# Heads laid out as 64 partitions of seven rows, with all attention products in quarters of the array

## The chip, the cores and the metric

The kernel runs on one core of one Trainium2 chip. TensorE multiplies matrices on a 128 x 128 array, VectorE (DVE), ScalarE (ACT) and GpSimd (POOL) work on vectors, and SyncE (SP) issues transfers, which sixteen DMA engines carry out. Each engine works through its instructions in order. The metric is device time in microseconds (us), from the start of an execution to its end. Lower is better.

## The reference

Attention for 8 batches of 12 heads with a sigmoid in place of a softmax, and then a gated feed-forward block over all 3584 tokens:

```python
# q, k, v: (8, 12, 448, 64)
scores = q @ k^T / sqrt(64) - log(448)
attn = 1 / (1 + exp(-scores))
x = (attn @ v), heads put side by side    # (3584, 768)
g = x @ w_gate                            # (768, 1536)
h = g * sigmoid(g) * (x @ w_val)
out = h @ w_out                           # (3584, 768)
```

A head has 448 rows, which is three and a half times 128, or seven times 64. Keys can be taken in any order, as long as k and v have the same one, and so can queries, as long as the rows of the output are put back where they belong.

## The kernel before, in words

Work is cut into 24 items of four heads: item i holds group i mod 3 of batch i div 3. For an item, q, k and v are loaded as float32 by SP, cast to 16 bits (by DVE for items 0 to 2, by POOL later), and q and k are transposed, for items 0 to 5 on TensorE (L371, copied out of PSUM by DVE at L377) and from item 6 on by a DMA transpose that SP issues (L387).

The first 384 rows of a head lie as 128 partitions of three rows (`load_main`, L261). The last 64 rows, the tails, are loaded apart (`tails`, L221 and L242): five DMAs for every item of batches 0 and 1, and nine in one block for a whole later batch. Their casts go to places in the tile `src16` that was set to zero at the start (L183), so that two heads' tails share one tile with zeros in the unused quarters.

Scores are computed with the keys on the partitions. One tile holds the scores of 128 keys of two heads against all 448 queries: two matmuls in the two row halves of the array (L411, `burst`), each with 64 rows of contraction, 128 columns of weights and 448 columns that stream. Six such tiles, and one tile for the tails of four heads from two full-array matmuls (L426, `burst_tail`), make an item. ScalarE applies the sigmoid to each tile (L434), seven per item. Values (`pv`) take 12 matmuls in the two column halves of the array (L447) and four in its quarters for the tails (L455). The result is copied from PSUM as `xT`, already transposed for what follows.

The feed-forward part runs per batch over twelve column blocks f (`f1`, L493, six matmuls each for the gate and the value), then per pair of batches over 14 units (`f2`, L551, twelve matmuls of 384 columns each). Weights are loaded by SP in four chunks w0 to w3 of six DMAs (L331), and w_out as twelve DMAs (wo, L354), and cast by POOL.

The order of the work is written by a planner inside the program (`list_schedule`). Operations are listed item by item, in four slots sl 0 to 3 per item, each with an engine, a planned duration and what it depends on. The planner walks through time, lets each engine take the first ready operation of a window (40 operations on PE, 8 on POOL, 1 on SP), and the instructions are then written out in that order. On the chip, an engine doesn't leave its order: an instruction that isn't ready holds all behind it. A planned DMA takes `n / 16 * max(0.042, 0.0105 + size / 27200)` us for n pieces of size bytes, one after the other, and lands 2.2 us later. SP's order of loads at the start is ORDER, q1 q2 w0 q3 w1 q4 w2 q5 w3 q6, where q1 stands for q, k and v of item 1. Later, item i's slot 1 brings the transpose of item i + 2, the loads of item i + 3, and for i from 4 to 7 three loads of wo. From item 3 on an item brings feed-forward products: three each for items 3 to 6, later up to two per slot.

Buffers are rings with a number of places: ten float32 loads (`st`), two of `src`, three of the transposed `qkT`, ten of sigmoid results (`pt`), and in PSUM two score tiles (A), two banks for transposes and values (TO), two for feed-forward products (G).

Of the kernel before, what the change touches and what calls it, by code (L numbers as in the profile page):

```python
# [25 lines left out]
class Op:  # L26


    def __init__(self, eng, dur, fn, deps=(), mode=("F", "F"), take=(), give=(), desc=(0, 0)):
        self.eng, self.dur, self.fn, self.mode = eng, dur, fn, mode  # L30
        self.deps = [d for d in deps if d is not None]
        self.take = [Slot(t) for t in take]
        self.give = list(give)
        self.rank = self.t0 = self.t1 = None
        n, size = desc
        self.hold = n == 2048
        self.dma = 2.2 if n == 2048 else n / 16 * max(0.042, 0.0105 + size / 27200)
# [97 lines left out]
def kernel(  # L135
# [17 lines left out]
    SM = 384  # L153
    ST = S - SM
    NS = SM // 128
# [14 lines left out]
    slots = {"A": 2, "TO": 2, "G": 2, "st": 10, "sq": 2, "sk": 2, "sv": 2, "src": 2,  # L170
# [6 lines left out]
    src16 = [one.tile([128, 2, 8, 128], BF16, tag=f"src{i}", name=f"src{i}") for i in range(NSRC)]  # L177
    NVB = 3
    vt16 = [one.tile([128, 2, D], FP16, tag=f"vt{i}", name=f"vt{i}") for i in range(NVB)]
    nc.gpsimd.memset(sb_t, sbias)  # L180
    make_identity(nc, idn)
    for t in src16:
        nc.vector.memset(t, 0.0)  # L183
# [27 lines left out]
    def tails(b, rs, eng="SP"):  # L211

        h0, h1 = 4 * rs[0], 4 * rs[-1] + 4
        first = rs[0] == 0
        nh = h1 - h0

        def qpart():
            if first:
                T["sq", b] = stg.tile([128, H, D], FP32, tag="sq", bufs=2, name=f"sq{b}")
            r = slice(0, 64) if b % 2 == 0 else slice(64, 128)  # L220
            (nc.scalar if eng == "ACT" else nc.sync).dma_start(  # L221
                out=T["sq", b][r, h0:h1], in_=q[b][h0:h1, SM:S, :].rearrange("h p d -> p h d"))
        a = op(eng, 0.6, qpart, take=["sq"] if first else [], desc=(64 * nh, D * 4))
        if first:
            R["sq", b, "slot"] = a.take
        for r in rs:
            R["sq", b * QB + r] = [a]

        def part(nm, src, hp, e, eng):
            n = len(rs)  # L230

            def fn():
                if hp == 0 and e in (None, 0) and first:
                    T[nm, b] = stg.tile([128, QB, 2, D], FP32, tag=nm, bufs=2, name=f"{nm}{b}")
                o = T[nm, b][64 * hp:64 * hp + 64, rs[0]:rs[-1] + 1]
                hs = slice(0, 4, 3) if hp == 0 else slice(1, 3)
                i_ = src[b][h0:h1, SM:S, :].rearrange("(r f) p d -> p r f d", f=4)[:, :, hs, :]
                if n == 1:
                    o, i_ = o[:, 0], i_[:, 0]
                else:  # L240
                    o, i_ = o[:, :, e], i_[:, :, e]
                (nc.scalar if eng == "ACT" else nc.sync).dma_start(out=o, in_=i_)  # L242
            return op(eng, 0.6, fn, take=[nm] if hp == 0 and e in (None, 0) and first else [],
                      desc=(64 * n * (2 if e is None else 1), D * 4))
        for nm, src in (("sk", k), ("sv", v)):
            g = eng if nm == "sk" else "SP"
            a = [part(nm, src, hp, e, g) for hp in range(2) for e in ((None,) if len(rs) == 1 else (0, 1))]
            if first:
                R[nm, b, "slot"] = a[0].take
            for r in rs:  # L250
                R[nm, b * QB + r] = a

    def load_main(i, nm, src, part=None):
        b, r = divmod(i, QB)

        def fn():
            if part in (None, 0):
                T["st_" + nm, i] = stg.tile([128, 4, NS, D], FP32, tag="st", bufs=10,
                                            name=f"st_{nm}{i}")
            h0, h1 = (0, 4) if part is None else (2 * part, 2 * part + 2)  # L260
            nc.sync.dma_start(  # L261
                out=T["st_" + nm, i][:, h0:h1],
                in_=src[b][4 * r + h0:4 * r + h1, 0:SM, :].rearrange("h (p s) d -> p h (s d)", s=NS))
        n = 4 if part is None else 2
        R["st_" + nm, i, part] = op("SP", 0.5, fn, take=["st"] if part in (None, 0) else [],
                                    desc=(128 * n, NS * D * 4))

    def groups(b, nm):

        if nm == "k":  # L270
            return 0, 3
        return (4, 7) if b % 2 == 0 else (5, 4)

    def cast_qk(i, nm, pp, eng):
        g = groups(i // QB, nm)[0]

        def fn():
            o = src16[i % NSRC][:, pp, g:g + NS, :].rearrange("p s (h d) -> p s h d", h=2)
            cp(eng, o, T["st_" + nm, i][:, 2 * pp:2 * pp + 2].rearrange("p h s d -> p s h d"))
        ld = R.get(("st_" + nm, i, None)) or R["st_" + nm, i, pp]  # L280
        ld0 = R.get(("st_" + nm, i, None)) or R["st_" + nm, i, 0]
        R["c" + nm, i, pp] = op(eng, 0.55 if eng == "DVE" else 0.48, fn, deps=[ld], take=["src"] if nm == "q" and pp == 0 else [],
                                give=ld0.take if pp else [])

    def cast_v(i, eng, part=None):
        def fn():
            if part in (None, 0):
                T["v16", i] = sb.tile([128, 4, NS, D], FP16, tag="v16", bufs=slots["v16"],
                                      name=f"v16_{i}")
            h0, h1 = (0, 4) if part is None else (2 * part, 2 * part + 2)  # L290
            cp(eng, T["v16", i][:, h0:h1], T["st_v", i][:, h0:h1])
        last = part in (None, 1)
        R["v16", i, part] = op(
            eng, 0.83 if part is None else 0.43, fn, deps=[R["st_v", i, part]],
            take=["v16"] if part in (None, 0) else [],
            give=(R.get(("st_v", i, None)) or R["st_v", i, 0]).take if last else [])

    def cast_tails(i, eng="POOL"):
        b, r = divmod(i, QB)
        gq, gk = groups(b, "q")[1], groups(b, "k")[1]  # L300

        def fq():
            ps = slice(0, 64) if b % 2 == 0 else slice(64, 128)
            cp(eng, src16[i % NSRC][ps, :, gq, :],
               T["sq", b][ps, 4 * r:4 * r + 4, :].rearrange("p (a h) d -> p a (h d)", a=2))

        def fk():
            for rh in range(2):
                ps = slice(64 * rh, 64 * rh + 64)
                for pp in range(2):  # L310
                    hp = rh ^ pp
                    cp(eng, src16[i % NSRC][ps, pp, gk, 64 * hp:64 * hp + 64],
                       T["sk", b][ps, r, pp, :])
        free = r == QB - 1
        R["tails", i] = [
            op(eng, 0.36, fq, deps=R["sq", i] + [R["cq", i, 0]], give=R["sq", b, "slot"] if free else []),
            op(eng, 0.8, fk, deps=R["sk", i] + [R["cq", i, 0]], give=R["sk", b, "slot"] if free else [])]

    def cast_vtail(i):
        b, r = divmod(i, QB)  # L320

        def fvt():
            nc.gpsimd.tensor_copy(out=vt16[i % NVB], in_=T["sv", b][:, r])
        R["vbd", i] = op("POOL", 0.3, fvt,
                         deps=R["sv", i] + ([R["pv", i - NVB]] if i >= NVB else []),
                         give=R["sv", b, "slot"] if r == QB - 1 else [])

    def load_w(w, dst, c, j2, nm):
        def fl():
            T[nm, c, j2] = stg.tile([128, 2, CW], FP32, tag="st", bufs=10, name=f"st_{nm}{c}_{j2}")  # L330
            nc.sync.dma_start(  # L331
                out=T[nm, c, j2],
                in_=w[j2 * 256:(j2 + 1) * 256, c * CW:(c + 1) * CW].rearrange(
                    "(j p) f -> p j f", p=128))
# [16 lines left out]
    def load_wo(f):  # L351
        def fl():
            T["wo", f] = stg.tile([128, DM], FP32, tag="st", bufs=10, name=f"st_wo{f}")
# [9 lines left out]
    def qkT_tile(i):  # L363
        T["qkT", i] = sb.tile([128, 2, 8 * 128], BF16, tag="qkT", bufs=slots["qkT"], name=f"qkT_{i}")

    def tr_pe(i, pp):

        def fpe():
            ps = T["tr", i, pp] = psum.tile([128, 8 * 128], BF16, tag="TO", bufs=2, name="ps_tr")
            for g in range(8):  # L370
                nc.tensor.transpose(out=ps[:, g * 128:(g + 1) * 128],  # L371
                                    in_=src16[i % NSRC][:, pp, g, :], identity=idn)

        def fm():
            if pp == 0:
                qkT_tile(i)
# [378 lines left out]
```

## Time and profile before

| what | value |
|---|---|
| median of three runs | 454.06 us (452.81 to 454.94) |
| the profiled execution's own time | 452.38 us |
| its span in the profile | 450.6 us |
| TensorE clock granted | 1.0 |
| PE busy | 431.1 us, 96% of the span |
| ACT / DVE / POOL busy | 224.6 / 173.6 / 134.4 us |
| DMA packets | 106656, of which 59520 under 512 B |
| read from HBM, written | 47.19 MB, 11.01 MB |

The profile describes one execution. A group of instructions has its busy time, the mean duration of one, and the idle time of its engine just ahead of it with what ended that. Matmuls overlap in the array, so the duration of one (about 350 ns for 448 columns) is longer than the step from one start to the next; the steps are what count. The chain of waits is followed back from the last instruction, each time to whatever released the one before. "Landing" is the time from the issue of a transfer to its arrival.

### The profile page before, as it was taken

Reading aid. Unit: us, or ns where it says so; the run is one execution under the profiler, and the core shown is the slowest. Engines: PE = TensorE matmul, PEld = TensorE weight load, DVE = VectorE, ACT = ScalarE, POOL = GpSimd, SP = SyncE. Lnnn points to the kernel's source line nnn. Section 1 sums busy time; section 2 is a strip of 40 time slices with the busy share of each in tenths; the row PEclk is TensorE's granted clock in tenths of the full one; section 3 lists DMA queues with packets and bytes.
Section 4 is the critical chain, followed back from the end, with each engine's and each line's share of the span. In section 5 each row is a group of like instructions: output and inputs, shape, how many; then the busy total and the mean of one; then the engine's idle time right before and its main releaser. Section 6 shows DMA issues by size and latency. Waiting matters only on the chain.

```text
span 450.6 us, 6887 instructions
## 1 busy us (share of the span) xinstructions
PE 431.1 (96%) x2640; PEld 209.7 (47%) x2640; DVE 173.6 (39%) x289; ACT 224.6 (50%) x304; POOL 134.4 (30%) x313
## 2 busy tenths in 40 slices
PE   3789999999899999999999999999999999999996
PEld 1334444444354444544445444444455445554563
DVE  4525554444334334334343333433433333334210
ACT  3787753677645465454663455554743643112111
POOL 3468563554742431344033303413100000000000
PEclk9999999999999999999999999999999999999999
DMA  6999896999977678765584627616300001010032
GB/s 158 322 339 277 250 276 169 289 250 240 280 177 215 153 188 133 185 167 166 103 178 146 153 72 203 185 29 162 81 36 1 36 35 36 35 71 0 36 105 105
DMA packets 106656, 68.08 MB, mean 151 GB/s; under 512 B 59520, under 2 KB 102784, under 8 KB 106624
## 3 DMA queue, kind: packets, MB, share of 16 engines
q1 hardware_dynamic: 104576, 60.44, 50.6%
q0 software_dynamic: 1488, 7.08, 4.8%
q8 instruction: 20, 0.33, 0.3%
q10 hardware_dynamic: 560, 0.13, 0.1%
q14 instruction: 12, 0.10, 0.1%
HBM read 47.19 MB, written 11.01 MB: 129 GB/s over the span
## 4 chain that ended last, share of the span: by engine, by line
PE 72%; DMA 17%; SPq 4%; POOL 2%; issue 1%; DVE 1%; ACT 1%; POOLq 0%
PE ps_o L551 19%; PE ps_g L493 18%; PE ps_v L493 18%; DMA st_wv<-in_moe_w_val_dram 6%; PE ps_ol L551 5%; PE ps_sc L411 5%; PE ps_pv L447 4%; DMA st_q<-in_q_dram 3%; DMA st_wo<-in_moe_w_out_dram 3%; DMA sv<-in_v_dram 2%; SPq L242 2%; POOL src L205 1%; DMA st_wg<-in_moe_w_gate_dram 1%; PE ps_sct L426 1%; SPq L261 1%
## 5 line engine op out<-in xcount | busy, mean ns | idle before, releaser
L434 ACT ACTIVATE pt<-ps_sc,sbiast 128x896 f16<-128x896 f32 x144 | 136.9, 1006 | 18.6 <-PE ps_sc L411 18.5
L493 PE MATMUL ps_g<-xT,wg 128*128 128x448 f16 x576 | 124.9, 353 | 1.7 <-DVE t L503 1.5
L493 PE MATMUL ps_v<-xT,wv 128*128 128x448 f16 x576 | 125.6, 353 | 0.5 <-POOL wv L337 0.5
L499 ACT ACTIVATE s<-ps_g 128x448 f16<-128x448 f32 x96 | 52.3, 545 | 128.9 <-PE ps_g L493 125.6
L503 DVE TENSOR_TENSOR t<-ps_g,s 128x448 f16<-128x448 f32 x96 | 59.9, 624 | 140.5 <-ACT s L499 140.3
L551 PE MATMUL ps_o<-wo,hT 128*128 128x384 f16 x528 | 92.3, 326 | 0.0
L551 PEld LDWEIGHTS <-hT 128*128 128x128 f16 x672 | 65.7, 98 | 45.9 <-issue 0.4
L493 PEld LDWEIGHTS <-wg 128*128 128x128 f16 x576 | 55.3, 98 | 56.3 <-issue 8.0
L493 PEld LDWEIGHTS <-wv 128*128 128x128 f16 x576 | 51.5, 98 | 60.8 <-issue 18.8
L509 DVE SCALAR_TENSOR_TENSOR hT<-ps_v,t 128x448 f16<-128x448 f32 x96 | 60.0, 625 | 51.1 <-PE ps_v L493 49.0
L411 PE MATMUL ps_sc<-qkT 64*128 64x448 bf16 x288 | 42.5, 364 | 5.5 <-ACT pt L434 2.9
L205 POOL CAST src<-st_q 128x384 bf16<-128x384 f32 x42 | 20.5, 510 | 90.0 <-DMA st_q<-in_q_dram 83.3
L447 PE MATMUL ps_pv<-pt,v 128*64 128x448 f16 x288 | 33.4, 362 | 0.6 <-ACT pt L434 0.6
L562 ACT ACTIVATE osb<-ps_o 128x384 f32<-128x384 f32 x22 | 10.8, 491 | 43.0 <-PE ps_o L551 43.0
L203 DVE CAST xT<-ps_pv 128x448 f16<-128x448 f32 x40 | 23.6, 620 | 20.0 <-PE ps_pv L455 20.0
L205 POOL CAST v<-st_v 128x768 f16<-128x768 f32 (+1 forms) x25 | 20.0, 801 | 25.6 <-issue 15.0
L434 ACT ACTIVATE pt<-ps_sct,sbiast 128x896 f16<-128x896 f32 x24 | 24.1, 1004 | 6.3 <-PE ps_sct L426 6.3
L564 DVE TENSOR_SCALAR osb<-ps_o 128x384 f32<-128x384 f32 x22 | 12.3, 557 | 36.6 <-PE ps_o L551 36.6
L576 POOL DMA_DIRECT2D out_dram<-osb x15 | 8.3, 555 | 57.6 <-DVE osb L564 38.4
L411 PEld LDWEIGHTS <-qkT 64*128 64x128 bf16 x288 | 9.1, 94 | 34.1 <-issue 30.2
L551 PE MATMUL ps_ol<-wo,hT 128*128 128x384 f16 x144 | 24.7, 326 | 0.0
L447 PEld LDWEIGHTS <-v 128*64 128x64 f16 x288 | 14.3, 110 | 17.3 <-issue 10.1
(34 smaller groups left out, 163.2 us busy)
## 6 DMA issues: line engine op xcount, KB each, us to landing
st_q<-in_q_dram SPq DMA_DIRECT2D x23, 384.0 KB, 4.0
st_k<-in_k_dram SPq DMA_DIRECT2D x23, 384.0 KB, 4.5
st_v<-in_v_dram SPq DMA_DIRECT2D x23, 384.0 KB, 5.2
out_dram<-osb POOLq DMA_DIRECT2D x15, 384.0 KB, 2.9
st_wg<-in_moe_w_gate_dram SPq DMA_DIRECT2D x12, 384.0 KB, 6.5
st_wv<-in_moe_w_val_dram SPq DMA_DIRECT2D x12, 384.0 KB, 8.3
st_wo<-in_moe_w_out_dram SPq DMA_DIRECT2D x12, 384.0 KB, 6.6
out_dram<-osb SPq DMA_DIRECT2D x8, 384.0 KB, 2.3
```

The source lines that it names most:

```text
L203: nc.vector.tensor_copy(out=o, in_=i)
L205: nc.gpsimd.tensor_copy(out=o, in_=i)
L411: nc.tensor.matmul(out=sc[:, hp, 0:S], lhsT=kT[r, s * 128:(s + 1) * 128], rhs=qT[r, :], start=True, stop=True)
L434: nc.scalar.activation(out=pt, in_=T[("sc",) + key][:, :, 0:S], func=SIGM, bias=sb_t, scale=qkscale)
L447: nc.tensor.matmul(out=ps[64 * hp:64 * hp + 64, :], lhsT=T["v16", i][:, 2 * pp + hp, s, :], rhs=T["pt", i, pp, s][:, hp, :], start=(s == 0 ...
L493: nc.tensor.matmul(out=T[nm, b, f], lhsT=w[c][:, j, ff * 128:(ff + 1) * 128], rhs=T["xT", b, j], start=(j == 0), stop=(j == KC - 1))
L499: nc.scalar.activation(out=t, in_=T["g", b, f], func=SIGM)
L503: nc.vector.tensor_tensor(out=t, in0=T["g", b, f], in1=T["s16", b, f], op=MULT)
L509: nc.vector.scalar_tensor_tensor(out=T["hT", m, f][:, o * S:(o + 1) * S], in0=T["v", b, f], scalar=HSC, in1=T["t1", b, f], op0=MULT, op1=MULT)
L551: nc.tensor.matmul(out=o, lhsT=T["hT", m, f][:, t * 128:(t + 1) * 128], rhs=wo16[f][:, cs], start=(f == 0), stop=(f == NF - 1))
L562: nc.scalar.activation(out=T["osb", m, t][:, c], in_=o, func=COPY, scale=HREC)
L564: nc.vector.tensor_scalar_mul(T["osb", m, t][:, c], o, HREC)
```

## The change

A head's 448 rows now lie as 64 partitions of seven rows: row 7p + s of the head is at partition p, slot s. Two heads lie on partitions 0 to 63 and two on 64 to 127. There are no tails, no zeroed places, and no separate tile for them.

- Loads: q, k and v of an item take two DMAs each, one for each half of the partitions, with pieces of 1792 bytes.
- Casts: one per tensor and item instead of two, plus those of the tails; for item 0 they are split by slots between DVE and ACT.
- Transposes: seven 128 x 128 blocks for q and seven for k, each on its own, instead of eight for each pair of heads; the DMA transpose has 1792 pieces instead of 2048.
- Scores: a tile holds one slot s of the keys of all four heads. Four matmuls in the array's four quarters fill it. There are seven tiles per item, all of one kind, and from item 3 on they are issued in pairs; as seven is odd, two items share seven pairs, one of which takes the last tile of one item and the first of the next.
- Values: four matmuls in the quarters for each of seven slots.
- Output: a tile of 128 tokens is stored by two DMAs of 64 partitions.

```diff
-        self.hold = n == 2048
-        self.dma = 2.2 if n == 2048 else n / 16 * max(0.042, 0.0105 + size / 27200)
+        self.hold = n == 1792
+        self.dma = 2.0 if n == 1792 else n / 16 * max(0.042, 0.0105 + size / 27200)
...
-    slots = {"A": 2, "TO": 2, "G": 2, "st": 10, "sq": 2, "sk": 2, "sv": 2, "src": 2,
+    slots = {"A": 2, "TO": 2, "G": 2, "st": 11, "src": 2,
              "v16": 3, "qkT": 3, "pt": 10, "xT": 14, "osb": 2}
...
-    for t in src16:
-        nc.vector.memset(t, 0.0)
...
+    def load(i, nm, src):
+
+        b, r = divmod(i, QB)
+
+        def part(g):
             def fn():
...
+                if g == 0:
+                    T["st_" + nm, i] = stg.tile([128, 2, NS, D], FP32, tag="st", bufs=slots["st"],
+                                                name=f"st_{nm}{i}")
+                h = 4 * r + 2 * g
+                nc.sync.dma_start(
+                    out=T["st_" + nm, i][64 * g:64 * g + 64],
+                    in_=src[b][h:h + 2].rearrange("a (p s) d -> p a s d", s=NS))
+            return op("SP", 0.5, fn, take=["st"] if g == 0 else [], desc=(128, NS * D * 4))
+        R["st_" + nm, i] = [part(0), part(1)]
...
+    def burst(ds):
+
 
         def fpe():
-            for pp, s in ds:
+            for i, s in ds:
                 sc = psum.tile([128, 2, 512], FP32, tag="A", bufs=2, name="ps_sc")
...
+                qT, kT = T["qkT", i][:, 0], T["qkT", i][:, 1]
+                for g in range(2):
+                    for a in range(2):
+                        r = slice(64 * a, 64 * a + 64)
+                        nc.tensor.matmul(
+                            out=sc[64 * g:64 * g + 64, a, 0:S].rearrange("k (s p) -> k s p", s=NS),
+                            lhsT=kT[r, s, 64 * g:64 * g + 64], rhs=qT[r, :, 64 * g:64 * g + 64],
+                            start=True, stop=True)
...
-    def burst_tail(i):
...
+                for s in range(s0, s1):
+                    for g in range(2):
+                        for a in range(2):
+                            nc.tensor.matmul(
+                                out=T["pv", i, g][64 * a:64 * a + 64, :],
+                                lhsT=T["v16", i][64 * g:64 * g + 64, a, s, :],
+                                rhs=T["pt", i, s][64 * g:64 * g + 64, a, :],
+                                start=(s == 0), stop=(s == NS - 1))
...
+                for n in range(2):
+                    bb, s = divmod(2 * t + n, NS)
+                    rows = slice((2 * m + bb) * S, (2 * m + bb + 1) * S)
+                    dma.dma_start(out=out[rows, c].rearrange("(p s) d -> s p d", s=NS)[s],
+                                  in_=T["osb", m, t][64 * n:64 * n + 64, c])
...
+    loads(0)
+    op("ACT", 1.5, lambda: nc.scalar.activation(out=warm, in_=sb_t, func=SIGM))
+    cast_qk(0, "q", None, [("DVE", 0, 4), ("ACT", 4, NS)])
+    tr_pe(0, 0)
+    cast_qk(0, "k", None, [("DVE", 0, 4), ("ACT", 4, NS)])
+    tr_pe(0, 1)
+    cast_v(0, "POOL")
...
+    def bursts(i, sl):
+
+        if i >= NQ:
+            return []
+        if i < QB:
+            return [[(i, s)] for s in range(2 * sl, min(2 * sl + 2, NS))]
+        if (i - QB) % 2 == 0 and i + 1 < NQ:
+            return [[(i, 2 * sl), (i, 2 * sl + 1)]] if sl < 3 else [[(i, 6), (i + 1, 0)]]
+        if (i - QB) % 2 == 0:
+            return [[(i, s) for s in range(2 * sl, min(2 * sl + 2, NS))]]
+        return [[(i, 2 * sl + 1), (i, 2 * sl + 2)]] if sl < 3 else []
```

## The prediction

> **What bounds the kernel now.** I read the chain of waits first, to see what kind of work ends last, then a table of stretches, then the order of matmuls on TensorE.
>
> ```profile
> PE 72%; DMA 17%; SPq 4%; POOL 2%; issue 1%; DVE 1%; ACT 1%; POOLq 0%
> ```
>
> ```profile
> 33.00:87.00 54.00, 52.33 (x340) 24.70 (x341) 27.10 (x45) 32.20 (x44) 34.34 (x68) 1.00 0.89 254
> 87.00:115.00 28.00, 26.45 (x170) 11.24 (x167) 12.77 (x21) 20.54 (x26) 14.27 (x30) 1.00 0.92 240
> 115.00:375.00 260.00, 259.69 (x1576) 125.37 (x1577) 96.88 (x160) 137.18 (x186) 69.86 (x175) 1.00 0.52 132
> ```
>
> In the stretches (length, busy PE, PEld, DVE, ACT, POOL, clock, DMA share, GB/s) TensorE is full from 115 us on, with DMA at half. Before 115 us DMA is at 0.9: there TensorE is full only because products of the feed-forward part stand in the gaps that late attention leaves. DMA and TensorE bound that stretch together. At 113 us the products run out, and the chain in order of time shows TensorE held by a transpose that stood behind loads in SP's queue:
>
> ```profile
> 104.47 5.57 DMA st_wo<-in_moe_w_out_dram
> 110.04 5.08 DMA qkT<-src
> 115.11 0.05 issue
> 115.16 0.38 PE ps_sc L411 x2
> ```
>
> Inside the full stretch, TensorE in order of time:
>
> ```profile
> 154.50 0.54 PE L426 MATMUL ps_sct<-qkT 128*128 128x448 bf16 x2
> 154.88 1.30 PE L493 MATMUL ps_v<-xT,wv 128*128 128x448 f16 x6
> 156.02 1.30 PE L493 MATMUL ps_g<-xT,wg 128*128 128x448 f16 x6
> 157.25 0.55 PE L411 MATMUL ps_sc<-qkT 64*128 64x448 bf16 x4
> 157.73 1.31 PE L493 MATMUL ps_v<-xT,wv 128*128 128x448 f16 x6
> ```
>
> A full-array matmul of 448 columns takes a step of 0.189 us (0.38 for the two tail products). Four half-array score matmuls take 157.73 - 157.25 = 0.48 for two steps: two halves run at once. The product before should have ended at 156.02 + 6 x 0.189 = 157.15, so the change of array shape costs 0.10 going in and 0.10 coming out, plus 0.01 at each first step: 0.21 per burst.
>
> **What the Trainium skill says.** TensorEngine Tiling (Array Packing), Key Properties: changing the tiling mode drains the array. The trace agrees, at about 0.095 us a change. TensorE: Matmul & The Clock Gate, Part 3, says that weights load under running matmuls only where the row group differs; the trace differs: the full-height column halves of L447 load under running matmuls and hold steps of 0.189 to 0.190. SBUF — State Buffer, Door 1 (the port swizzle): partitions 0 to 63 reach 8 of 16 DMA ports, so 64 partitions move 196 GB/s against 328 for 128 at 1 MiB, and two transfers to the two halves together are only 6% faster. The trace has this only for stores:
>
> ```profile
> out_dram<-osb POOLq DMA_DIRECT2D x15, 384.0 KB, 2.9
> out_dram<-osb POOLq DMA_DIRECT2D x6, 192.0 KB, 3.7
> ```
>
> ```profile
> 440.40:441.40 1.00, 1.00 (x8) 0.59 (x6) 0.00 (x0) 0.49 (x1) 0.00 (x0) 1.00 0.94 372
> 436.90:438.40 1.50, 1.50 (x11) 0.92 (x10) 0.00 (x0) 0.49 (x1) 0.00 (x0) 1.00 0.97 246
> ```
>
> Half the bytes take longer to land when they leave 64 partitions, and SP's stores move 372 GB/s from 128 partitions but 246 where the tile goes out in two halves (packets of 3072 B take a median 214 ns there, 124 in the other).
>
> **The change, part by part.**
>
> Scores. Before, one item has six half-array steps and two tail steps; after, seven quarter-array steps: 0.189 us less. Only L455 runs in quarters before:
>
> ```profile
> L447 PE MATMUL ps_pv<-pt,v 128*64 128x448 f16 x288 | 33.4, 362 | 0.6 <-ACT pt L434 0.6
> L455 PE MATMUL ps_pv<-pt,vt 64*64 64x448 f16 x96 | 9.2, 373 | 0.0
> ```
>
> Its four matmuls start within 10 ns; from their start to the next full product is 0.316 us = 0.189 + 0.095 drain + 0.03. So I take 0.189 per step and 0.23 per burst. A run of several quarter steps is not shown; below zero is excluded, since every step still streams 448 columns; above, 0.024 per step (the delay of the first column-split step, 0.213 against 0.189) would cost 336 x 0.024 = 8 us, and weights that cannot load ahead (about 0.10) 34 us. I take 0, as L447 loads ahead.
>
> Bursts. Three per item before plus a tail burst without a change of shape; after 3.5. Shape changes for scores: 3.5 x 0.23 - 3 x 0.21 = +0.17. Values: seven steps both times, but three shape changes become two: a lone block costs 0.353 above its steps before and 0.23 after, -0.12. Where scores and values stand side by side (ten blocks before) they now share the shape, about -0.1 more. Sum per item -0.189 + 0.17 - 0.12 - 0.05 = about -0.2 us. For the 15 items whose scores start after 115 us: -3.0 us.
>
> Loads. One item's q, k and v are 1.376 MB. Before: 1536 packets of 768 B at a median 36 ns and 768 of 256 B at 18 (the trace's packet records), over 16 engines: 3.5 + 0.9 = 4.4 us, 4.7 with their spread. After: 768 packets of 1792 B, all to 64 partitions. From above, the full rate seen for weight loads, 375 GB/s, gives 3.7 us; from below, 218 GB/s (eight ports, the page's asymptote) gives 6.3. I take 231 GB/s, the stores' 393 KB in 1.7 us: 5.96 us. SP issues six DMAs per item; before, three, plus five for each item of the first two batches or nine once per later batch: about 6 per item as well, but the block of nine (97.4 to 102.7 us, DMA share about 0.4) is gone. The DMA transpose shrinks from 2048 to 1792 packets, some 0.3 us.
>
> Start. With first packets at 1.7 us, item 0's k lands near 6.4 instead of 4.7; cast, seven transposes and copy bring the first sigmoid to about 9.5 instead of 7.65. But then no second half is waited for, and 21 sigmoids at 0.96 to 1.0 end near 31, before 31.9: about -0.7, used up by the next item.
>
> Loads against the written order. The planner prices such a load at 8 x 0.0764 = 0.611 us, 3.67 an item, and fixes TensorE's order by it; I take 2.3 us more. Landing times, adding 5.96 per item and 6.3 per weight chunk (six of 1.05) in ORDER from 1.7: k4 42.2, k5 54.4, the last weights 62.7, k6 66.6. With 0.7 landing and 0.94 cast, the transposes of item 4 can end on TensorE at about 44, where the planner's sum has the cast near 34.5, a few us after item 3 starts. TensorE stands in order behind them: products, scores and the values of the item before, which also wait through the new burst that pairs an item's last tile with the next item's first. From item 6 on: its casts end at 68.3, its transpose starts some 1.7 later and moves for 2.3; then loads of item 7 (5.96), three wo (3.15) and the transpose of 7 (2.3), landed (0.8) at about 84.5. By then the order holds f 0 to 11 (27.2), scores of 3 to 6 (8.4), three values blocks (4.7) and transposes (2.4), less 1.5 done early: 41 us of work between 33 and 84.5, so 10 us idle where before had 1.7 in 54. Items 7 and 8 then take 11 products x 2.27 + 2 x 3.65 = 32.3, to 116.8, and the values of item 8 and one product more, to 120.6. Before stood at the same place at 115.2: +5.4 us. The stall at 113 is inside this difference.
>
> POOL: casts of q, k, v and tails were 4 x 0.51 + 0.40 + 4 x 0.23 + 0.83 + 0.30 = 4.5 us an item; three of 896 elements, by the slope from 384 (0.51) to 768 (0.83), are 2.8. Hidden: POOL waits 83 us for q loads already. The removed memsets (1.8 on VectorE) end before q lands. Stores become two per tile, on POOL (0.55 each) free in that stretch; on SP at the end the second issue delays the last landing by about 0.6.
>
> Sum against the execution's own 452.38 (span 450.6): 5.4 - 3.0 + 0.6 = +3.0, 455.4. The median of the runs is 1.7 above that execution, so 457.
>
> **The rivals.**
>
> 1. Likeliest, half-port loads met by an order made for fast ones: 457, own range 454 to 462. Break-even is an item load of about 5.6 us.
> 2. Loads to the two halves overlap and run at the full rate, 3.7 us. Then the order fits, the stall at 113 (1.9) and most of 1.5 us of smaller ones go, the start gives 1, scores and values 0.2 x 21 = 4.2: 454.06 - 8 = 446. For: several DMAs queue at once. Against: the two stores above did too.
> 3. Loads are slow, but feed-forward products stand early enough in TensorE's order to cover half of the 10 us: 457 - 5 = 452.
> 4. Quarter steps do not load ahead fully: 0.024 each on top of the first case, in the full stretch (15 x 14 steps, 5 us) and part of the rest: 464. Against: L447.
>
> **How the numbers follow.** Chances 0.50, 0.20, 0.18, 0.12. About 0.5% (451.8 to 456.3) is what a measurement of this kernel can tell from no change. Faster: the second and a third of the third, 0.26. Same: the rest of the third and a fifth of the first, 0.22. Slower: 0.52. The range reaches from the second case to the fourth, 446 to 465.
>
> **What would show it.** The load packets at 120 to 130 ns and q/k/v landing later than 4.0 to 5.2 us after issue; DMA share near 1 with under 270 GB/s between 12 and 65 us; TensorE idle by several us before transposes (L371's) and scores between 36 and 87 us, ended by DMA or POOL casts; score bursts of two steps near 0.61 from shape to shape, values blocks near 1.55 instead of 1.67; TensorE full again from about 87 us. The prediction is wrong if load packets take 80 ns, if TensorE's idle time before 115 us stays under 4 us, or if quarter steps are far from 0.189.

## The result, and the profile after

| | before | after |
|---|---|---|
| median | 453.44 us (451.92 to 454.94) | 460.59 us (459.17 to 461.01) |
| ratio, with its 95% interval | | 1.0152 (1.0109 to 1.0196) |
| profiled execution, own time | 452.38 us | 460.97 us |
| its span | 450.6 us | 459.2 us |
| POOL busy | 134.4 us | 109.6 us |
| DMA packets | 106656 | 65348 |
| granted TensorE clock, mean | 1.0 | 0.988 |

The change costs 7 us (1.5%). The forecast was 457.0, a loss of 3 from the 454.06 known then: the right sign and inside the range, but less than half of the loss. The kernel before varies with its clock: over 88 executions in the series of this document, those with a mean clock of 0.998 or more have a median of 452.7 us, those with 0.996 or less 455.3, and the profiled one, with 1.0, belongs to the first kind.

The chain of waits of the kernel after, as shares of its span (DMA was at 17%):

```profile
PE 75%; DMA 19%; SPq 3%; POOL 1%; DVE 1%; ACT 1%; issue 0%; POOLq 0%
```

The same chain in order of time (start, length, what it was), only its long transfers between 13 and 62 us:

```profile
13.34 8.04 DMA st_v<-in_v_dram
...
21.40 11.45 DMA st_q<-in_q_dram
...
32.91 8.80 DMA st_wv<-in_moe_w_val_dram
...
41.73 9.92 DMA st_v<-in_v_dram
...
51.66 10.56 DMA st_q<-in_q_dram
```

Until 62 us the time is set by transfers one after another, the loads of q, k and v among them. The table of stretches (length, busy PE, PEld, DVE, ACT, POOL, clock, DMA share, GB/s), for the three that were shown of before:

```profile
33.00:87.00 54.00, 41.63 (x364) 19.27 (x363) 20.81 (x34) 29.09 (x39) 27.78 (x32) 0.91 0.94 245
87.00:115.00 28.00, 26.52 (x221) 11.82 (x214) 12.93 (x21) 17.98 (x24) 12.93 (x15) 1.00 1.13 258
115.00:375.00 260.00, 260.00 (x1994) 126.69 (x1993) 100.59 (x165) 139.37 (x190) 59.44 (x80) 1.00 0.65 131
```

From 33 to 87 us TensorE now idles 12.4 us where it idled 1.7 before. The 28 us after that are as full as before (1.5 us idle in both), and the long stretch is full in both. TensorE in order of time shows where the idle time is (in brackets: idle before it, and what ended that):

```profile
38.17 1.30 PE L384 MATMUL ps_g<-xT,wg 128*128 128x448 f16 x6 [0.38 <-DVE t L394]
48.38 0.93 PE L284 MATMUL ps_tr<-idn,src 128*128 128x128 bf16 x7 [8.91 <-POOL src L199]
49.10 2.45 PE L384 MATMUL ps_v<-xT,wv 128*128 128x448 f16 x6
51.48 0.78 PE L317 MATMUL ps_sc<-qkT 64*64 64x448 bf16 x8
52.19 1.31 PE L384 MATMUL ps_g<-xT,wg 128*128 128x448 f16 x6
53.34 0.55 PE L284 MATMUL ps_tr<-idn,src 128*128 128x128 bf16 x7
```

One wait holds most of it: 8.91 us before the transposes of item 4's q (L284, before L371). POOL's order shows what they waited for:

```profile
43.63 0.83 POOL L250 CAST wv<-st_wv 128x768 f16<-128x768 f32 x1 [1.04 <-DMA st_wv<-in_moe_w_val_dram]
45.54 0.83 POOL L250 CAST wv<-st_wv 128x768 f16<-128x768 f32 x1 [1.08 <-DMA st_wv<-in_moe_w_val_dram]
47.39 0.93 POOL L199 CAST src<-st_q 128x896 bf16<-128x896 f32 x1 [1.02 <-DMA st_q<-in_q_dram]
49.91 0.93 POOL L199 CAST src<-st_k 128x896 bf16<-128x896 f32 x1 [1.59 <-DMA st_k<-in_k_dram]
```

POOL waits before every one of these casts: the weights and then q and k of item 4 come late from the DMA engines. The table of stretches for the end of that wait, and for two of the microseconds of work behind it:

```profile
45.00:48.30 3.30, 0.00 (x0) 0.00 (x0) 0.00 (x0) 0.00 (x0) 1.74 (x2) 0.50 1.04 231
50.00:52.00 2.00, 2.00 (x13) 0.49 (x10) 0.92 (x2) 0.00 (x0) 1.05 (x2) 0.51 1.06 340
```

In the wait the DMA engines are all busy (share 1.04) and move 231 GB/s. And TensorE's clock has gone to half: the six matmuls at 49.10 take 2.45 us instead of 1.30. The trace's record of the clock has it at half from 41.7 to 52.0 us; the wait began at 39.5.

The quarter products themselves, in the full stretch:

```profile
150.71 1.30 PE L384 MATMUL ps_g<-xT,wg 128*128 128x448 f16 x6
151.94 0.57 PE L317 MATMUL ps_sc<-qkT 64*64 64x448 bf16 x8
152.44 1.31 PE L384 MATMUL ps_v<-xT,wv 128*128 128x448 f16 x6
...
156.67 1.30 PE L384 MATMUL ps_v<-xT,wv 128*128 128x448 f16 x6
157.90 0.57 PE L317 MATMUL ps_sc<-qkT 64*64 64x448 bf16 x8
158.30 1.49 PE L348 MATMUL ps_pv<-pt,v 64*64 64x448 f16 x28
159.73 1.31 PE L384 MATMUL ps_g<-xT,wg 128*128 128x448 f16 x6
```

The product at 150.71 is through at 150.71 + 6 x 0.189 = 151.84; the next begins at 152.44, so a burst of two quarter steps takes 0.60, that is 2 x 0.189 and 0.22 for going in and out. A burst and a values block side by side follow a product that is through at 156.67 + 6 x 0.189 = 157.80. They take 159.73 - 157.80 = 1.93: nine steps of 0.189 and again 0.23, once for both. In the page's groups (busy, mean ns of one, idle time before them) the quarters stand so:

```profile
L317 PE MATMUL ps_sc<-qkT 64*64 64x448 bf16 x672 | 52.3, 375 | 6.0 <-ACT pt L331 3.4
...
L348 PE MATMUL ps_pv<-pt,v 64*64 64x448 f16 x672 | 38.6, 360 | 0.6 <-ACT pt L331 0.5
```

One takes as long as a matmul of L447 or L455 before. The landing times of the loads, by the page's list of transfers (KB each, median us from issue to landing):

```profile
st_q<-in_q_dram SPq DMA_DIRECT2D x48, 224.0 KB, 4.9
```

For q 384 KB landed in 4.0 before; now 224 KB take 4.9. The median is over the whole run, most of it with little else in transfer, and hides what happens before 62 us.

Where the 7 to 9 us come from, by the start of the same piece of work in both traces. The count f runs over the feed-forward products in the order of the kernel, twelve per batch:

| start of | before | after | after - before |
|---|---|---|---|
| first sigmoid | 7.7 | 10.2 | +2.5 |
| 21st sigmoid | 30.9 | 32.0 | +1.1 |
| f 12 (batch 1) | 74.2 | 88.3 | +14.1 |
| f 24 (batch 2) | 115.6 | 127.8 | +12.2 |
| f 48 | 220.9 | 231.0 | +10.1 |
| f 72 | 325.4 | 334.2 | +8.8 |
| f 95 (the last) | 416.9 | 424.8 | +7.9 |
| last unit of w_out products | 444.5 | 452.4 | +7.9 |
| end of the span | 450.6 | 459.2 | +8.6 |

The loss is there by f 12, with 14.1 us. From f 12 to f 24, where the kernel before stands in its stall at 113, 1.9 come back; from f 24 to f 95 the quarter products give back 4.3, and the end takes 0.7. A part of this is only a shift of work: ahead of f 24 stand two bursts of item 9 after (1.20 us by the step above) and one before (0.48). Without it the loss at f 24 is 11.4, and 3.5 come back later.

### The profile page after: what moved, and what is told of

The parts are those of the page before. It is cut to its first block, busy times and chain, and to the rows that moved or that the text cites. A ratio compares the mean times of both kernels' runs of the same rounds, so it can differ in the third digit from the quotient of the medians.

```text
span 459.2 us, 7942 instructions
## 1 busy us (share of the span) xinstructions
PE 427.3 (93%) x3252; PEld 211.7 (46%) x3252; DVE 168.9 (37%) x278; ACT 225.1 (49%) x305; POOL 109.6 (24%) x145
## 2 busy tenths in 40 slices
DMA packets 65348, 66.97 MB, mean 146 GB/s; under 512 B 36640, under 2 KB 61472, under 8 KB 65312
## 4 chain that ended last, share of the span: by engine, by line
PE 75%; DMA 19%; SPq 3%; POOL 1%; DVE 1%; ACT 1%; issue 0%; POOLq 0%
PE ps_g L384 20%; PE ps_v L384 20%; PE ps_o L442 19%; DMA st_v<-in_v_dram 7%; PE ps_sc L317 6%; PE ps_pv L348 5%; PE ps_ol L442 5%; DMA st_q<-in_q_dram 5%; DMA st_wv<-in_moe_w_val_dram 3%; DMA st_k<-in_k_dram 3%; SPq L215 2%; DMA qkT<-src 1%; DVE t L394 1%; ACT s L390 1%; POOL v L199 0%
## 5 line engine op out<-in xcount | busy, mean ns | idle before, releaser
L331 ACT ACTIVATE pt<-ps_sc,sbiast 128x896 f16<-128x896 f32 x168 | 159.3, 1005 | 38.7 <-PE ps_sc L317 38.6
L317 PE MATMUL ps_sc<-qkT 64*64 64x448 bf16 x672 | 52.3, 375 | 6.0 <-ACT pt L331 3.4
L463 POOL DMA_DIRECT2D out_dram<-osb x36 | 18.7, 525 | 112.6 <-issue 77.7
L199 POOL CAST src<-st_q 128x896 bf16<-128x896 f32 x21 | 19.6, 934 | 85.2 <-DMA st_q<-in_q_dram 84.2
L348 PE MATMUL ps_pv<-pt,v 64*64 64x448 f16 x672 | 38.6, 360 | 0.6 <-ACT pt L331 0.5
L317 PEld LDWEIGHTS <-qkT 64*64 64x64 bf16 x672 | 14.4, 107 | 38.6 <-issue 33.3
L199 POOL CAST v<-st_v 128x896 f16<-128x896 f32 x24 | 22.4, 935 | 38.6 <-DMA st_v<-in_v_dram 23.5
L453 ACT ACTIVATE osb<-ps_o 128x384 f32<-128x384 f32 x22 | 10.8, 490 | 39.8 <-PE ps_o L442 39.8
L348 PEld LDWEIGHTS <-v 64*64 64x64 f16 x672 | 19.8, 109 | 16.0 <-issue 4.8
L284 PE MATMUL ps_tr<-idn,src 128*128 128x128 bf16 x84 | 8.6, 258 | 19.2 <-POOL src L199 10.7
L442 PE MATMUL ps_ol<-wo,hT 128*128 128x384 f16 x144 | 24.7, 326 | 0.0
L455 DVE TENSOR_SCALAR osb<-ps_o 128x384 f32<-128x384 f32 x22 | 12.3, 557 | 31.8 <-PE ps_o L442 31.8
```

Of the source, the lines that this page charges most:

```text
L199: nc.gpsimd.tensor_copy(out=o, in_=i)
L317: nc.tensor.matmul(out=sc[64 * g:64 * g + 64, a, 0:S].rearrange("k (s p) -> k s p", s=NS), lhsT=kT[r, s, 64 * g:64 * g + 64], rhs=qT[r, :, ...
L331: nc.scalar.activation(out=pt, in_=T[("sc",) + key][:, :, 0:S], func=SIGM, bias=sb_t, scale=qkscale)
L348: nc.tensor.matmul(out=T["pv", i, g][64 * a:64 * a + 64, :], lhsT=T["v16", i][64 * g:64 * g + 64, a, s, :], rhs=T["pt", i, s][64 * g:64 * ...
L442: nc.tensor.matmul(out=o, lhsT=T["hT", m, f][:, t * 128:(t + 1) * 128], rhs=wo16[f][:, cs], start=(f == 0), stop=(f == NF - 1))
L455: nc.vector.tensor_scalar_mul(T["osb", m, t][:, c], o, HREC)
```

## The experiments

**Theory.** Loads to 64 partitions are slow, the planner believes them to be fast, and the written order holds TensorE behind item 4's transposes. The first question was whether it is the loads or the order: a square of four kernels, with loads to halves or to all partitions, and with the order made for fast or for slow loads.

*The planner's price for such a load.*

```diff
-  self.dma = 2.0 if n == 1792 else n / 16 * max(0.042, 0.0105 + size / 27200)
+  self.dma = 2.0 if n == 1792 else n / 128 * 0.993 if size == 1792 else n / 16 * max(0.042, 0.0105 + size / 27200)
```

> The changed kernel with one number of the planner altered: a load of half the partitions (128 pieces of 1792 B) is priced at 0.993 us instead of 0.611, so that the written order reckons with 231 GB/s. Loads and all other work stay. If the idle time of TensorE comes from an order written for fast loads (the prediction's step), products move ahead of the late transposes and of the 12.4 us idle between 33 and 87 us at most 5 are left: 454 us, from 451 to 456. If the loads' volume alone sets the pace of the first 87 us, whatever the order, nothing is won: 459 to 461.

*Each load fills all 128 partitions.* The price, and so the written order, stays. Heads 1 and 2 of each group of four then stand in each other's place in the output; the amount of work is the same.

```diff
-  out=T["st_" + nm, i][64 * g:64 * g + 64],
-  in_=src[b][h:h + 2].rearrange("a (p s) d -> p a s d", s=NS))
+  out=T["st_" + nm, i][:, g],
+  in_=src[b][h:h + 2].rearrange("a (p s) d -> (a p) s d", s=NS))
```

> The changed kernel with the same number of load DMAs, the same piece count and piece size, but each DMA fills one slot pair of all 128 partitions instead of both of 64: the destination is [:, g] and not [64g:64g+64]. Heads 1 and 2 of each group of four thereby change places in the rows of x, with the weights left as they are; the amount of work is the same. If half of the partitions is what makes a load slow, a piece takes 74 to 85 ns instead of a median 134, an item's loads move at 350 GB/s or more, TensorE idles under 3 us between 33 and 87 us, and the time is 446 us (444 to 449). If instead the number of DMAs or their issue time on SP (six times 0.65 us per item) is the cause, it stays at 459 to 461.

*Both edits.*

> Both edits: loads to all 128 partitions, but an order written for slow ones (0.993 us per DMA). Heads 1 and 2 of each group of four change places in x, as in the run with whole-partition loads alone. If only the match of order and loads matters, this mismatch costs as well: some 3 us above the run with fast loads and the fast price. If late loads are the cause and the order only amplifies them, loads that come early cost nothing: within 1.5 us of that run, about 447.

*A version that puts the heads back:* q and k in one transfer of 128 partitions each, v in one of 128 and two of 64 (these two are a sixth of the bytes, and the planner's price for them is 1.625 times as high, which the lines below leave out); the second index a of the tile then says which half a head's partner is in, and the quarters are chosen to fit.

```diff
+  if ah is None:
+      nc.sync.dma_start(out=o, in_=hs.rearrange("(a g) (p s) d -> (g p) a s d", g=2, s=NS))
+  else:
+      nc.sync.dma_start(out=o[ps, ah], in_=hs.rearrange("g (p s) d -> (g p) s d", s=NS))
...
-  out=sc[64 * g:64 * g + 64, a, 0:S].rearrange("k (s p) -> k s p", s=NS),
+  out=sc[64 * (a ^ g):64 * (a ^ g) + 64, a, 0:S].rearrange("k (s p) -> k s p", s=NS),
...
-  out=T["pv", i, g][64 * a:64 * a + 64, :],
-  lhsT=T["v16", i][64 * g:64 * g + 64, a, s, :],
-  rhs=T["pt", i, s][64 * g:64 * g + 64, a, :],
+  out=T["pv", i, a][64 * g:64 * g + 64, :],
+  lhsT=T["v16", i][64 * (a ^ g):64 * (a ^ g) + 64, a, s, :],
+  rhs=T["pt", i, s][64 * (a ^ g):64 * (a ^ g) + 64, a, :],
```

> A kernel that keeps the reference's output: q and k of an item in one DMA each over all 128 partitions (head 2a + g at partition half g), v as one DMA over 128 partitions for two heads and two DMAs of 64 partitions for the other two, scores and values in quarters chosen to fit. SP issues five DMAs per item instead of six. By the theory of the half partitions, one item's loads take 1.22 + 1.22 + 0.61 + 1.0 = 4.05 us instead of 5.96, close to the 4.7 of the kernel before, and the time is 447 us (445 to 450), below both kernels. If quarter products cost more than they save in the full stretch, it ends above 452.

Measured (kernel before in the same series: 454.84 us):

| loads | order for fast loads | order for slow loads |
|---|---|---|
| to half the partitions | after: 460.59, ratio 1.0152 | 457.70, 1.0065 (1.0024 to 1.0105) |
| to all partitions | 443.60, 0.9715 (0.9655 to 0.9776) | 445.70, 0.9763 (0.9703 to 0.9823) |
| the version that puts the heads back | 443.64, 0.9717 (0.9657 to 0.9776) | |

The loads decide: the same bytes, the same number of transfers, the same pieces of 1792 bytes, with 128 partitions in each instead of 64, take 17 us off and turn a loss of 1.5% into a gain of 2.8% by the ratio, 2.5% by the medians. The order made for slow loads wins 2.9 us by the medians where the loads are slow (0.6%, or 0.9% by the ratios) and loses 2.1 where they are fast. The 454 us expected of it alone did not come, and the loss of 2.1 lies between the two answers that were expected: so the order matters by itself, but much less than the loads. The stretches of the kernel with loads to all partitions:

```profile
33.00:87.00 54.00, 53.59 (x475) 24.91 (x472) 27.30 (x45) 39.89 (x51) 32.70 (x38) 1.00 1.01 315
...
115.00:375.00 260.00, 260.00 (x1985) 127.56 (x1984) 99.87 (x164) 135.21 (x184) 49.94 (x70) 1.00 0.46 108
```

TensorE is full from 33 us on, its clock whole, and its loads come at 315 GB/s instead of 245. Item 4's transposes run at 39.53 with no idle time before them:

```profile
39.53 0.55 PE L284 MATMUL ps_tr<-idn,src 128*128 128x128 bf16 x7
```

In the packet records, the pieces of 1792 bytes take a median 74 ns here (mean 87), and 134 in the kernel after (mean 127). The re-priced order does not remove the idle time, it spreads it. First its stretch, then two lines of TensorE's order:

```profile
33.00:87.00 54.00, 45.26 (x385) 20.68 (x385) 23.17 (x38) 31.62 (x41) 26.91 (x31) 1.00 0.99 246
```

```profile
59.24 0.55 PE L384 MATMUL ps_v<-xT,wv 128*128 128x448 f16 x2 [1.38 <-POOL wv L250]
73.64 0.55 PE L384 MATMUL ps_v<-xT,wv 128*128 128x448 f16 x2 [1.32 <-POOL wv L250]
```

8.7 us of idle time are left, where 5 at most were expected, at the same 246 GB/s. Of these, 3.5 now stand before products whose weights are late, 2.1 before transposes and 3.1 before other work. The longest gap is 1.38 us, and the clock stays at 1.00. So the order was an amplifier (3 us), and the slow rate of the loads was the cause.

**Is there a threshold?** The prediction put a break-even at an item load of 5.6 us; the test's idea was that below it the order would fit. Two doses between the ends tell a threshold from a proportion: v alone to halves (a third of the bytes; the diff below), and q and k alone to halves (two thirds; the same with the condition turned round).

```diff
-  nc.sync.dma_start(
-      out=T["st_" + nm, i][64 * g:64 * g + 64],
-      in_=src[b][h:h + 2].rearrange("a (p s) d -> p a s d", s=NS))
+  if nm == "v":
+      nc.sync.dma_start(
+          out=T["st_" + nm, i][64 * g:64 * g + 64],
+          in_=src[b][h:h + 2].rearrange("a (p s) d -> p a s d", s=NS))
+  else:
+      nc.sync.dma_start(
+          out=T["st_" + nm, i][:, g],
+          in_=src[b][h:h + 2].rearrange("a (p s) d -> (a p) s d", s=NS))
```

> A dose of the half-partition loads: q and k fill all partitions, v fills halves, six DMAs per item as before. Heads 1 and 2 of each group of four exchange their v and their place in x; the amount of work is the same. An item's loads then take 2 x 1.22 + 1.99 = 4.4 us. The prediction put the break-even with the kernel before at about 5.6 us per item, with TensorE's products as cover below that: 444 to 446 us. If the cost is proportional to the share of half-partition bytes, a third of 17: 449.

> The larger dose: q and k fill halves, v all partitions. Heads 1 and 2 of each group of four exchange their v and their place in x; the amount of work is the same. An item's loads take 2 x 1.99 + 1.22 = 5.2 us. With a threshold near 5.6 us it would end at 447 to 452, below the kernel before; proportional, two thirds of 17 above 443.6: 455.

| share of the bytes in half loads | median less that of the kernel before | ratio | f 12 starts at | TensorE busy, 33 to 87 us |
|---|---|---|---|---|
| none | -11.2 us | 0.9715 (0.9655 to 0.9776) | 73.1 | 53.59 |
| a third (v) | -3.3 us | 0.9938 (0.9911 to 0.9965) | 80.3 | 47.44 |
| two thirds (q, k) | +1.1 us | 1.0026 (1.0002 to 1.0049) | 85.3 | 43.98 |
| all (after) | +7.2 us | 1.0152 (1.0109 to 1.0196) | 88.3 | 41.63 |

The threshold's answers did not come. The proportion's came to within 3 us, and the first third loses even more than the later ones (7.9, 4.4 and 6.1 us). With v alone in halves the same gate shows in TensorE's order:

```profile
41.71 0.93 PE L289 MATMUL ps_tr<-idn,src 128*128 128x128 bf16 x7 [6.16 <-POOL src L199]
```

After this wait the clock is at half for the first 3.6 us of work, 1.8 us of the first third's loss. A sixth of the bytes in halves, in the version that puts the heads back, costs nothing (443.64 against 443.60), but that version has one transfer fewer per item and its order is priced for its half loads, so it is no clean dose. Between a third and the whole the loss grows roughly in proportion; where below a third it sets in is not shown. The pieces of 1792 bytes took a mean of 98 and 120 ns with one third and two thirds in halves, so an item load (768 pieces on 16 engines) took about 4.7 and 5.8 us: the place where the change breaks even lies between. The predicted 5.6 is inside, neither confirmed nor excluded; what failed is the idea that the order fits below it: at 4.7 TensorE still stood for 6.16 us.

**The new pair of bursts.** The prediction named the burst that joins an item's last tile and the next item's first as a second way in which lateness passes on. Here all bursts stay inside an item, once on the version with whole loads and once on the kernel after.

```diff
-  if (i - QB) % 2 == 0 and i + 1 < NQ:
-      return [[(i, 2 * sl), (i, 2 * sl + 1)]] if sl < 3 else [[(i, 6), (i + 1, 0)]]
-  if (i - QB) % 2 == 0:
-      return [[(i, s) for s in range(2 * sl, min(2 * sl + 2, NS))]]
-  return [[(i, 2 * sl + 1), (i, 2 * sl + 2)]] if sl < 3 else []
+  return [[(i, s) for s in range(2 * sl, min(2 * sl + 2, NS))]]
```

> The whole-partition kernel that keeps the reference's output, with bursts that stay inside an item (2, 2, 2 and 1 tiles) instead of the pair that takes the last tile of one item and the first of the next: ten more changes of array shape and back, the same steps. The prediction priced one burst's changes at 0.23 us, so 443.6 + 2.3 = 446 us. If a change of shape is hidden by other work, or if the planner sets the odd tile beside a values block, it stays within 1 us of 443.6.

> The changed kernel (loads of half the partitions) with bursts inside an item. If the pair across two items adds to the early idle time, because values of item i wait through it for the transposes of item i + 1, then the early stretch gains more than the 2.3 us that ten more changes of shape cost: below 459. If the coupling costs nothing, 460.6 + 2.3 = 463 us.

On whole loads 448.27 us (0.9878, 0.9815 to 0.9942), on half loads 463.89 (1.0233, 1.0163 to 1.0304). On whole loads f 24 to f 95 grows from 297.0 to 299.3 us: ten more bursts of 0.23 are 2.3, so that price holds. The rest of the 4.6 us is lost early, where the price said nothing: TensorE is busy 23.84 of the 27 us from 33 to 60 instead of 25.66, and f 24 starts 2.1 later. On half loads f 24 starts at 127.4 against 127.8 in the kernel after, so the joined bursts cost next to nothing there. It is 3.3 us slower by the medians; in the profiled executions the span grows by 1.8, and the full stretch by 2.3. The joined burst is not a cause of the loss.

**Which partitions make a load slow?** A kernel of loads alone, one execution: six stretches of 2.75 MB in twelve transfers with pieces of 1792 bytes.

> Loads by themselves; the kernel computes nothing of the reference and writes zeros. Six stretches of twelve DMAs, each DMA 128 pieces of 1792 B, 2.75 MB per stretch, with a wait between stretches. In order: all to partitions 0 to 63; in turn to 0 to 63 and 64 to 127; all to 32 to 95; all to 128 partitions (one piece each); halves in turn, the low half issued by SP and the high half by ACT; 128 partitions again. By the theory of the ports, what counts is whether the partitions span both sides of 64: the first and second stretch run at 220 to 235 GB/s with pieces near 130 ns, the third, 64 partitions as well, near 370 with pieces near 74 ns, as do the fourth and sixth; the fifth stays under 300. If 64 partitions are slow for another cause (fewer engines, two pieces per partition), the third is as slow as the first.

The table of stretches (length, busy DVE, POOL, clock, DMA share, GB/s), from inside the first five: partitions 0 to 63; the two halves in turn; partitions 32 to 95; all 128; the halves from two queues in turn, SP's and ACT's.

```profile
4.00:14.00 10.00, 3.67 (x11) 0.00 (x0) 1.00 1.08 203
20.00:29.00 9.00, 1.33 (x10) 0.00 (x0) 1.00 1.06 249
34.00:41.00 7.00, 2.36 (x17) 0.00 (x0) 1.00 0.95 301
45.00:53.00 8.00, 1.47 (x10) 0.00 (x0) 1.00 0.93 303
57.00:65.00 8.00, 1.33 (x9) 0.00 (x0) 1.00 1.07 259
```

64 partitions are not slow as such: 32 to 95 run like all 128, with pieces of a median 74 ns in both, against 151 for 0 to 63, 118 for the halves in turn and 114 from two queues. A transfer that lies half on each side of partition 64 is fast; 64 to 127 alone was not run, and the sixth stretch, 128 partitions again, ran into the stores of the end. The 370 GB/s expected of the fast stretches did not come. Their median hides some long pieces: from 45 to 53 us 41 of 1351 took over 100 ns, up to 1379, which makes the mean 87. Sixteen engines at 87 ns and a share of 0.93 give 307, near the 303; what makes those pieces long was not found. The Trainium skill's SBUF — State Buffer, Door 1 and "Can I just issue two DMAs to hit both halves?", gives 196 against 328 GB/s and 6% for two together; the run has 203 against 303, but the halves in turn gain 23%. That page's remedy, one transfer over all 128 partitions, is not the only one here.

**The end.** On the version with whole loads, the second store of the last tile goes to another queue, to take back the 0.7 us.

```diff
-  dma.dma_start(out=out[rows, c].rearrange("(p s) d -> s p d", s=NS)[s],
+  q_ = nc.scalar if end and n else dma
+  q_.dma_start(out=out[rows, c].rearrange("(p s) d -> s p d", s=NS)[s],
```

> The whole-partition kernel with the second store DMA of the very last output tile issued by ACT instead of SP, so that the two halves are issued side by side. From the start of the last output unit to the end of the span the kernel before took 6.1 us, the changed kernel and the whole-partition one 6.8; if the second issue on SP is what the end gained, 6.1 to 6.3 comes back and the time is 443.1 us. If the landing of two half-partition stores is the cause, nothing moves.

443.38 us (442.64 to 444.19), ratio 0.9757 (0.9726 to 0.9788). The last unit to the end of the span takes 6.5 us instead of 6.8; the medians can't tell a gain of that size.

**The block of tails.** The prediction gave the kernel before a handicap, the nine tail loads of a batch in one block at 97.4 to 102.7 us and the stall at 113. Here, in the kernel before, the tails of every item are loaded with the item.

```diff
-        if b < 2:
+        if b >= 0:
```

> The kernel before the change with the tails of every item loaded by five DMAs of its own, as it already does for the first two batches, instead of nine in one block per batch. If the block at 97 to 103 us is what holds the transpose that TensorE waits for at 113 us, the wait of 1.9 us goes and the time falls by about 2 us, to 452; that would be two fifths of the 4.9 us that the whole-partition kernel is ahead of it at the first product of batch 2. If the queue is only as late in another way (15 issues of tails per batch instead of 9), it stays at 454 or rises.

457.13 us (455.93 to 458.81), ratio 1.0053 (1.0032 to 1.0074): no gain of 2 us, but a loss, the second of the two answers expected. The stall before 115, 1.71 in the kernel before, shrinks to 0.37, and a longer one opens earlier, before another item's scores:

```profile
89.38 0.93 PE L411 MATMUL ps_sc<-qkT 64*128 64x448 bf16 x4 [2.56 <-DMA qkT<-src]
90.23 2.42 PE L493 MATMUL ps_g<-xT,wg 128*128 128x448 f16 x6
```

The wait moved and grew, and f 24 starts at 119.2 instead of 115.6. Some 1.6 us of that are the clock: its record is at half from 89.24 to 92.65, and the six matmuls take 2.42 us. So the block was no handicap that a change could simply cash in. What puts f 24 at 110.7 in the version with whole loads, 4.9 us ahead of the kernel before, was not taken apart (fewer packets, shorter casts on POOL, no tails); it stays open.

## Why the prediction was right, and where its sums were off

**Half loads met by an order made for fast ones** was the likeliest case, and it is what happened. Its estimate of 231 GB/s is the trace's figure, 233 and 231 from 6 to 18 us and 229 to 231 in the wait; its pieces of 120 to 130 ns measured a median 134, a mean 127. The idle time was put at 10 us before 84.5, with item 4's transposes in front of it; 12.4 were measured before 87, 8.9 of them there. Whole loads take it away.

**The early term was the mis-sized one:** +5.4 us up to f 24, and 12.2 measured, or 11.4 without the shifted burst. The prediction had f 24 at 120.6; it came at 127.8. Of those 7.2 us:

- 2.4 are more idle time between 33 and 87 us, and 1.5 are idle time from 87 to 115, which the sum had as full.
- 1.8 are the clock: TensorE worked at half speed from 48.4 to 52 us after its long wait, and no term had that.
- 1.2 are the two bursts of item 9 ahead of f 24, which the sum did not have there.
- 0.3 are left unassigned.

Behind the first of these is the step that failed most plainly, the landing times. They were added up in order, each transfer alone. By that sum the last weights of w1 land at 38.1, and k of item 4 at 42.2; POOL casts them at 45.5 and 49.9. Yet the bytes moved by 42 us, 10.8 MB (GB/s times length, summed from 1.7 us), are close to the 11.1 that the sum wanted. The transfers in flight share the engines, so that later ones take from earlier ones: when the last of w1 is cast, at 45.5, 11.6 MB have moved, though all that was issued up to it is 10.2. A load of q or k lands 10.6 to 11.5 us after its issue there (the chain, at 51.66 and 21.40), and item 4's transposes start at 48.4 and 53.3 instead of ending near 44. The weights are late with them, which is why a truer price in the planner helps so little.

**Start.** -0.7 was wrong in sign: the first sigmoid came at 10.2 instead of 9.5, and the 21st started 1.1 later than before. Its claim to be "used up by the next item" kept the error small.

**Full stretch.** -3.0 was somewhat too little: f 24 to f 95 takes 301.3 us before and 297.0 after, -4.3, of which 0.7 is the shifted burst. The bases held: 0.189 a step, 0.22 to 0.23 per burst. Counted by the time from each matmul's start to the next, the scores between f 24 and f 95 take 24.7 us instead of 27.0 (the shifted burst is in this), the values 21.6 instead of 23.6, and all other products 250.7 both times. A change of shape costs nearly the same for quarters as for halves (0.22 to 0.23 per burst against 0.21).

**POOL and the end.** The casts take 0.93 us each, 2.8 an item as worked out; POOL waits for loads all the same, so its 24.8 us less work bought no time in this kernel. The end: +0.6 predicted, +0.7 measured. The block of tail loads had a DMA share of 0.54 from 97.4 to 102.7 us, not about 0.4; the sum did not use it.

The sum of the terms as measured is 12.2 - 4.3 + 0.7 = 8.6, the growth of the span (450.6 to 459.2). The medians grew by 7.2, since the profiled execution of before lay 1.1 below its median and that of after 0.4 above.

**The rivals.** Loads that overlap at the full rate: the half loads did not do so, but the price for that case, 446, was near what whole loads gave, 443.6. Products that cover half of the idle time: no, 12.4 us of idle time stayed where that case had 5, and even the re-priced order, made for it, covers only 3.7 of them. Quarter steps that do not load ahead: no, they hold 0.189. The statement of the Trainium skill's TensorE: Matmul & The Clock Gate, Part 3, that a change of the row group is what lets weights load ahead, stays contradicted by L447 before, where halves by columns held that step (the same section also names a background weight buffer as a second way, which no run here tests); the score quarters after, whose row group changes from one to the next, say nothing for or against it.

**Break-even** at 5.6 us an item stays open: the two doses put it between 4.7 and 5.8.

## What to carry to other kernels

A layout that is better for the array can be paid for by the transfers that fill it: for each tile ask which partitions one transfer touches, and keep it half on each side of partition 64, even where the number of transfers and bytes doesn't change. Where the order is fixed ahead, add up what is in flight rather than landing times one by one, and count a long wait on TensorE at more than its length (8.9 us of wait cost another 1.8 here). The change and its loads are worth separating before a verdict: the quarters with whole loads are 2.5 to 2.8% faster than the kernel before, and with half loads 1.5% slower.

## What the runs showed of the hardware

- A load of 64 partitions runs as fast as one of 128 if it lies on partitions 32 to 95 (301 and 303 GB/s, pieces of 74 ns), and a third slower on 0 to 63 (203 GB/s, 151 ns). Two queues for the two halves gave 259 against 249 in turn from one.
- After 8.9 us without work TensorE's clock stood at 0.5, and the next 3.6 us of work ran at half speed (six matmuls in 2.45 us instead of 1.30). In the traces here a wait of 2.56 us (the tails of every item loaded with it) was enough to halve the clock, and waits of up to 1.71 us from 20 us on left it whole; after the five waits that halved it, half speed lasted another 3.0 to 5.8 us. The Trainium skill's TensorE: Matmul & The Clock Gate, Part 1, has the same halving after an idle window of about 3.4 us, and about 3.4 us of activity until it ends. The end is near that in four of the five; but the wait of 2.56 us was shorter than the page's window.
- Four matmuls of 64 x 64 weights in four quarters hold a step of 0.189 us over 28 matmuls in a row, the step of one matmul of the full array.
